# First halves of the next pass's tiles issued inside the attention, and output copies given to ScalarE there: a fused chunked-attention and snake-MLP kernel

## The chip, the cores and the metric

The kernel runs on one core of a Trainium2 chip. The metric is device time in microseconds (us) of the whole program. Six runs of the kernel before took 226.98 to 228.42 us, with a median of 227.48 us. One of the executions, the one that took 227.02 us, was also recorded by the hardware profiler. Its span from the first to the last instruction is 225.2 us, so 1.8 us lie around the span.

## The reference

Two operators follow one another. The first is attention in chunks: every chunk of 32 queries sees eight memory rows, 16 rows to its left, its own 32 and 8 to its right. The second is a two-layer MLP with the activation h + sin²(αh)/α.

```python
# B, H, S, D = 4, 8, 768, 64; chunk, left, right = 32, 16, 8
for c in range(S // chunk):
    l, r = max(0, c*chunk - left), min(S, (c+1)*chunk + right)
    kf = concat([mem_k, k[:, :, l:r]]); vf = concat([mem_v, v[:, :, l:r]])
    a = softmax(q_c @ kf.T / sqrt(D))
    out[:, :, c*chunk:(c+1)*chunk] = a @ vf
x = out.transpose(0, 2, 1, 3).reshape(3072, 512)
h = x @ w_in                       # 512 -> 2048
g = h + sin(alpha * h)**2 / (alpha + 1e-9)
return g @ w_out                   # 2048 -> 512
```

## The kernel before, in words

**Passes.** The batch has four elements, and each is a pass of 768 tokens: an attention that makes xT (the transposed attention output, 128 x 4 x 768, bf16), a first product with its activation (`layer`, 16 tiles of 128 hidden features each, which makes gT), and a second product (`second`, six output tiles of 128 tokens by 512). This text calls the attentions of passes 1, 2 and 3 A1, A2 and A3, and the layers after them layer 1, 2 and 3. Pass 0 has a different attention, `attention_first`, which the change doesn't touch.

**The order is written out by hand.** There is no scheduler: each engine executes its instructions in the order in which the program issues them. The second product is a generator, and `Feed.take(n)` issues its next n matmuls. So the second product of pass i runs in pieces inside the attention and the layer of pass i+1. In `attention` (line 448) the list `shares` says how many matmuls are taken in each step.

**A step of an attention.** Step s issues `scores(s)` (eight matmuls on TensorE and three exponentials on ScalarE, lines 270 and 283), half of the step's share of the feed, `values(s-2)` (eight matmuls, line 296, then a reciprocal and a multiplication on VectorE which make x_blk, lines 302 and 303), the other half of the share, and `turn_x(s-3)` (four transposes on TensorE, line 313, and a copy into xT on VectorE, line 316). There are eight blocks j = 0 to 7 of 96 tokens, and eleven steps. In A3 the first five blocks are not turned by TensorE: a transposing DMA, issued by SyncE (line 464), puts them into xT.

**A tile of a layer.** `first` issues `half_first` for tokens 0 to 383 (four matmuls, line 476, reading blocks 0 to 3 of xT) and for tokens 384 to 767 (blocks 4 to 7), then a sine on ScalarE (line 496). A square follows, on ScalarE (line 500) or on VectorE (line 503), as a string says: "VAVAVAVAAVAAVAVA" in layer 1, "AAAV" in layers 2 and 3. The fused multiply and add on VectorE that makes gT (line 506) is issued one tile later.

**PSUM.** There are eight banks. The planner `plan` gives names to sets of them, and `take_bank` hands out the one that was taken longest ago. In A1, A2 and A3, `big` holds three pairs of banks, which scores and values take in turn, and `one` holds two single banks. An output tile being accumulated keeps one of these (`kept`), and the transposes of `turn_x` use the other. The layer takes its pairs from `h`, which is `big`, and in layer 1 also the pair of `one`. A pair comes free when its last reader is done: the exponentials of line 283, the multiplication of line 303 or the fused add of line 506.

**Output tiles.** `end_o` (line 529) copies a finished bank into o_sb, which has two buffers. Even tiles are copied by VectorE (line 535), odd ones by ScalarE (line 537). SyncE then issues the output's DMA (line 538).

`ahead` (line 485) is already in the kernel: it takes a pair of `big`, issues the first half of tile ft into it and remembers the pair in `begun`, from which `layer` picks it up. Before, only `attention_first` calls it.

Of the kernel before, what the change touches and what calls it, by code (L numbers as in the profile page):

```python
# [42 lines left out]
def kernel(  # L43
# [17 lines left out]
    NJ = S // QW  # L61
# [17 lines left out]
    rings = {}  # L79

    def plan(**sets):
        for kind, ring in sets.items():
            rings[kind] = list(ring)
# [3 lines left out]
    def take_bank(kind):  # L87
        ring = rings[kind]
        bank = next(n for n in ring if n not in kept)
        ring.remove(bank)  # L90
        ring.append(bank)
        return bank

    def two(kind="big"):
        bank = take_bank(kind)
        return ps[:, bank:bank + 2, :]

    def single(kind="one"):
        return ps[:, take_bank(kind), :]

    def packed(bank, n, width):
        return bank.bitcast(BF)[:, 0:n * width].rearrange("p (n c) -> p n c", n=n)
# [54 lines left out]
    def cross_steps(b):  # L157
        for j in range(NJ):
            nc.sync.dma_start_transpose(kTs[b % 2][:, :, P * j:P * j + P], kst[:, j, :])
            yield  # L160
        for t in range(NSUB):
            nc.sync.dma_start_transpose(qTs[b % 2][:, :, P * t:P * t + P], qst[:, t, :])
            yield
# [31 lines left out]
    def send_memv(b):  # L195
        for j in range(NJ):
            nc.sync.dma_start(vws[b % 2][64:72, :, j, 0:D], memv_st[64:72, b])
# [62 lines left out]

    state = {"n": 0}

    def scores(b, j, kind="big"):
        pitch = 104 if b < 2 else P
        sc = two(kind)
        for hp in range(HP):
            for e in range(2):
                nc.tensor.matmul(  # L270
                    sc[:, e, QW * hp:QW * hp + QW],
                    kTs[b % 2][64 * e:64 * e + 64, hp, pitch * j:pitch * j + P],
                    qTs[b % 2][64 * e:64 * e + 64, hp, QW * j:QW * j + QW],
                )
        pt = pts[state["n"] % NPT]
        state["n"] += 1
        for m in range(3):
            col = m
            if j == 0 and m == 0:
                col = 3  # L280
            if j == NJ - 1 and m == 2:
                col = 4
            nc.scalar.activation(  # L283
                pt[:, 0:H * QW].rearrange("p (g e c) -> p g e c", g=2, e=4)[:, :, :, 32 * m:32 * m + 32],
                sc[:, :, 0:4 * QW].rearrange("p g (e c) -> p g e c", e=4)[:, :, :, 32 * m:32 * m + 32],
                ACTF.Exp, bias=biasm[:, col:col + 1], scale=0.125,
            )
        return pt

    def values(b, j, pt):  # L290
        ot = two()
        otv = ot[:, :, 0:4 * (D + 1)].rearrange("p e (g c) -> p e g c", c=D + 1)
        for e in range(2):
            for hp in range(HP):
                i = 4 * e + hp
                nc.tensor.matmul(  # L296
                    otv[:, e, hp, :], pt[:, QW * i:QW * i + P],
                    vws[b % 2][:, 2 * hp + e, j, 0:D + 1],
                )
        rinv = blk.tile([QW, 2, HP], F32, name="rinv")  # L300
        x_blk = blk.tile([QW, HP, 2, D], BF, name="x_blk", bufs=6)
        nc.vector.reciprocal(rinv[:], otv[0:QW, :, :, D])  # L302
        nc.vector.tensor_tensor(  # L303
            out=x_blk[:].rearrange("p g e d -> p e g d"), in0=otv[0:QW, :, :, 0:D],
            in1=rinv[:].unsqueeze(3).to_broadcast([QW, 2, HP, D]),
            op=ALU.mult,
        )
        return x_blk

    def turn_x(xT, j, x_blk):  # L310
        xtp = packed(single(), KT, QW)
        for kt in range(KT):
            nc.tensor.transpose(  # L313
                xtp[:, kt, :], x_blk[:, kt].rearrange("p e d -> p (e d)"), ident[0:QW, 0:QW]
            )
        nc.vector.tensor_copy(xT[:, :, QW * j:QW * j + QW], xtp)  # L316
# [131 lines left out]
    def attention(b, stream, shares, lag, crossed, beside=iter(()), beside_from=0):  # L448
        xT = xp.tile([P, KT, S], BF, name="xT")
        ptl, xbl = {}, {}  # L450
        for s in range(NJ + lag + 1):
            n = shares[s] if s < len(shares) else 0
            if s < NJ:
                ptl[s] = scores(b, s)
            if s == NJ - 1:
                nc.scalar.preload_act_table(ACTF.Sin)
            stream.take(n // 2)
            if s >= beside_from:
                next(beside, None)
            j = s - lag  # L460
            if 0 <= j < NJ:
                xbl[j] = values(b, j, ptl.pop(j))
                if j < crossed:
                    nc.sync.dma_start_transpose(
                        xT[:, :, QW * j:QW * j + QW], xbl.pop(j)[:].rearrange("p g e d -> p (g e d)")
                    )
            stream.take(n - n // 2)
            if crossed <= j - 1 < NJ:
                turn_x(xT, j - 1, xbl.pop(j - 1))
        return xT  # L470

    def half_first(hT, ft, hf, xT):
        for kt in range(KT):
            nc.tensor.matmul(  # L476
                hT[:, hf, 0:HALF],
                w_in_sb[:, kt, P * ft:P * ft + P],
                xT[:, kt, HALF * hf:HALF * hf + HALF],
                start=(kt == 0), stop=(kt == KT - 1),  # L480
            )
# [3 lines left out]
    def ahead(ft, hf, xT):  # L485
        if ft < 3:
            begun[ft] = two("big")
            half_first(begun[ft], ft, hf, xT)
# [24 lines left out]
    def second(i, gT, cut=0):  # L513

        def begin_o():
            bank = take_bank("one")
            kept.add(bank)
            return bank

        def part(s, bank, f0, f1):  # L520
            for ft in range(f0, f1):
                nc.tensor.matmul(  # L522
                    ps[:, bank, :], gT[:, ft, P * s:P * s + P], w_out_sb[:, ft, :],
                    start=(ft == 0), stop=(ft == FT - 1),
                )
                if ft < FT - 1:
                    yield

        def end_o(s, bank):
            kept.remove(bank)  # L530
            rings["one"].remove(bank)
            rings["one"].append(bank)
            o_sb = mlp.tile([P, d_model], F32, name="o_sb", bufs=2)
            if s % 2 == 0:
                nc.vector.tensor_copy(o_sb[:], ps[:, bank, :])  # L535
            else:
                nc.scalar.copy(o_sb[:], ps[:, bank, :])  # L537
            nc.sync.dma_start(out[S * i + P * s:S * i + P * s + P, :], o_sb[:])

        early = []  # L540
        if cut:
            for s in range(2):
                early.append(begin_o())
                yield from part(s, early[s], 0, cut)
        for s in range(NSUB):
            bank = early[s] if s < len(early) else begin_o()
            yield from part(s, bank, cut if s < len(early) else 0, FT)
            end_o(s, bank)
            yield
# [63 lines left out]
    xT = attention_first(kq, alphas, ahead)  # L613
# [62 lines left out]
    xT = attention(1, feed, (6, 8, 4, 4, 4, 3, 3, 3, 3, 1, 1), 2, 0, crossings, 3)  # L676
# [3 lines left out]
    for i in range(1, B):  # L680
        last = i == B - 1
        if i > 1:
            crossings = cross_steps(i + 1) if not last else iter(())

        def begin(ft, i=i):
            if ft == (2 if i > 1 else 0):
                for _ in crossings:
                    pass

        if i == 1:  # L690
            assert feed.left() == 16
            plan(h=rings["big"] + [min(rings["one"])])
            layer(i, xT, "VAVAVAVAAVAAVAVA", begin, 0)
            free = rings["h"]
            plan(one=(free[0], free[0] + 1), h=free[1:])
        else:
            plan(h=rings["big"])
            layer(i, xT, "AAAV", begin, feed.left() - (0 if last else 16))
        if not last:
            if i + 2 < B:  # L700
                load_rows(i + 2)
            plan(big=rings["h"])
            nc.scalar.preload_act_table(ACTF.Exp)
            feed.take(6)
            xT = attention(i + 1, feed, (4, 8, 4, 4, 3, 3, 3, 3, 4, 4, 4), 2, 5 if i == B - 2 else 0)
            if i + 2 < B:
                load_v(i + 2)
                send_memv(i + 2)
# [31 lines left out]
```

## Time and profile before

| | |
|---|---|
| median of six runs | 227.48 us (226.98 to 228.42) |
| profiled execution | 227.02 us, span 225.2 us |
| TensorE busy | 214.8 us, 95% of the span |
| ScalarE, VectorE, GpSimd busy | 151.7, 135.3, 84.2 us |
| granted TensorE clock, mean | 0.997 |
| A1, from its first score matmul to the first matmul of layer 1 | 61.32 to 78.20 us |
| layer 1, to the first matmul that follows it | 78.20 to 99.76 us |
| A2, likewise | 101.15 to 118.54 us |
| layer 2 | 118.54 to 148.65 us |
| A3 | 150.69 to 166.09 us |
| layer 3 | 166.09 to 199.60 us |
| last 100 matmuls of the second product | 199.60 to 221.27 us |

All positions are microseconds from the span's start, as the trace gives them. A row of the timeline has the start, the length, the engine, the line, what is computed and how many instructions are merged in it; in brackets stands how long the engine had been idle and which instruction ended that. A matmul's length includes the time until its result has arrived, so that matmuls which follow one another without a gap overlap in the rows. The time that a matmul takes of the engine is therefore read from start to start: eight matmuls of 128x384 from 118.71 to 120.04, some 0.163 us each, and 0.215 us for one of 128x512 (two from 120.04 to 120.47).

### The profile page before, as it was taken

Reading aid. Unit: us, or ns where it says so; the run is one execution under the profiler, and the core shown is the slowest. Engines: PE = TensorE matmul, PEld = TensorE weight load, DVE = VectorE, ACT = ScalarE, POOL = GpSimd, SP = SyncE. Lnnn points to the kernel's source line nnn. Section 1 sums busy time; section 2 is a strip of 40 time slices with the busy share of each in tenths; the row PEclk is TensorE's granted clock in tenths of the full one; section 3 lists DMA queues with packets and bytes.
Section 4 is the critical chain, followed back from the end, with each engine's and each line's share of the span. In section 5 each row is a group of like instructions: output and inputs, shape, how many; then the busy total and the mean of one; then the engine's idle time right before and its main releaser. Section 6 shows DMA issues by size and latency. Waiting matters only on the chain.

```text
span 225.2 us, 4455 instructions
## 1 busy us (share of the span) xinstructions
PE 214.8 (95%) x1720; PEld 115.9 (51%) x1720; DVE 135.3 (60%) x238; ACT 151.7 (67%) x222; POOL 84.2 (37%) x106
## 2 busy tenths in 40 slices
PE   7999999999998899999899999999999999999992
PEld 2555555555545555554555555544555555544440
DVE  5684748793526969995782775664743863771110
ACT  2559478894777579999856779798948678651011
POOL 7958843796979951175880000000000000000000
PEclk9999999999999999999999999999999999999998
DMA  5999999999999999999999954541330110111211
GB/s 79 163 117 136 170 210 208 206 204 139 93 209 168 130 118 175 117 138 132 159 177 102 99 104 93 103 156 54 68 108 3 47 47 0 48 51 47 93 66 74
DMA packets 94573, 25.97 MB, mean 115 GB/s; under 512 B 82632, under 2 KB 91480, under 8 KB 94552
## 3 DMA queue, kind: packets, MB, share of 16 engines
q0 software_dynamic: 71520, 14.81, 111.5%
q1 hardware_dynamic: 23032, 10.88, 23.7%
q8 instruction: 13, 0.21, 0.5%
q14 instruction: 8, 0.07, 0.2%
HBM read 29.67 MB, written 6.29 MB: 160 GB/s over the span
## 4 chain that ended last, share of the span: by engine, by line
PE 55%; DVE 8%; ACT 2%; issue 2%; DVEq 0%; ACTq 0%
PE ps L522 29%; PE ps L476 20%; DVE gT L506 3%; PE ps L270 2%; PE ps L296 2%; DVE u L503 2%; DVE x_blk L303 1%; ACT u L496 1%; PE ps L313 1%; ACT u L500 1%; DVE xT L316 1%; ACT o_sb L537 0%; DVE rinv L302 0%; DVE o_sb L535 0%; DVEq L506 0%
## 5 line engine op out<-in xcount | busy, mean ns | idle before, releaser
L522 PE MATMUL ps<-w_out_sb,gT 128*128 128x512 bf16 x384 | 99.3, 379 | 1.8 <-DVE o_sb L535 0.8
L476 PE MATMUL ps<-xT,w_in_sb 128*128 128x384 bf16 x512 | 90.0, 326 | 0.8 <-DVE gT L506 0.7
L506 DVE SCALAR_TENSOR_TENSOR gT<-u,inv_alpha,ps 128x768 bf16<-128x768 f32 x64 | 63.4, 1012 | 24.8 <-ACT u L500 20.6
L496 ACT ACTIVATE u<-ps,alpha_sb 128x768 f32<-128x768 f32 x64 | 57.0, 898 | 22.3 <-PE ps L476 21.2
L476 PEld LDWEIGHTS <-w_in_sb 128*128 128x128 bf16 x512 | 49.7, 98 | 37.6 <-issue 2.0
L522 PEld LDWEIGHTS <-gT 128*128 128x128 bf16 x384 | 34.2, 97 | 32.1 <-issue 2.1
L500 ACT ACTIVATE u<-u 128x768 f32<-128x768 f32 x40 | 33.7, 843 | 1.3
L283 ACT ACTIVATE pt<-ps,biasm 128x256 bf16<-128x256 f32 x72 | 28.7, 476 | 6.0 <-ACT pt L283 2.3
L535 DVE COPY o_sb<-ps 128x512 f32<-128x512 f32 x12 | 8.2, 687 | 24.8 <-PE ps L522 20.7
L537 ACT COPY o_sb<-ps 128x512 f32<-128x512 f32 x12 | 7.1, 589 | 22.2 <-PE ps L522 22.2
L503 DVE TENSOR_TENSOR u<-u 128x768 f32<-128x768 f32 x18 | 17.2, 954 | 6.0 <-ACT u L496 5.9
L303 DVE TENSOR_TENSOR x_blk<-ps,rinv 96x512 bf16<-96x512 f32 x24 | 16.5, 687 | 0.8
L144 POOL DMA_DIRECT2D kst<-in_k_dram x16 | 11.6, 724 | 9.9 <-DMA vw<-in_v_dram 4.4
L323 PE MATMUL ps<-idle 128*128 128x512 bf16 x39 | 13.7, 446 | 1.2 <-DVE vw L564 1.2
L139 POOL DMA_DIRECT2D kst<-in_k_dram x16 | 11.0, 686 | 7.7 <-DMA vw<-in_v_dram 5.5
L249 ACT COPY kT<-ps 128x672 bf16<-128x672 bf16 x8 | 5.8, 719 | 9.7 <-PE ps L234 6.8
L302 DVE RECIPROCAL rinv<-ps 96x8 f32<-96x8 f32 x24 | 4.9, 202 | 12.0 <-PE ps L296 6.1
L296 PEld LDWEIGHTS <-pt 128*128 128x128 bf16 x192 | 9.0, 98 | 4.8 <-issue 0.8
L503 POOL TENSOR_TENSOR u<-u 128x768 f32<-128x768 f32 x6 | 8.9, 1492 | 5.8 <-ACT u L496 5.8
L152 POOL DMA_DIRECT2D qst<-in_q_dram x12 | 10.5, 902 | 0.8 <-DMA kst<-in_k_dram 0.8
L296 PE MATMUL ps<-vw,pt 128*128 128x65 bf16 x192 | 9.8, 193 | 0.0
L270 PEld LDWEIGHTS <-kT 64*128 64x128 bf16 x192 | 4.9, 94 | 7.6 <-issue 7.0
(77 smaller groups left out, 154.0 us busy)
## 6 DMA issues: line engine op xcount, KB each, us to landing
out_dram<-o_sb SPq DMA_DIRECT2D x24, 256.0 KB
vw<-in_v_dram POOLq DMA_DIRECT2D x6, 384.0 KB, 13.4
w_out_sb<-in_moe_w_out_dram POOLq DMA_DIRECT2D x2, 1024.0 KB, 18.6
w_in_sb<-in_moe_w_in_dram POOLq DMA_DIRECT2D x3, 512.0 KB, 10.3
qst<-in_q_dram POOLq DMA_DIRECT2D x12, 128.0 KB, 6.4
kst<-in_k_dram POOLq DMA_DIRECT2D x14, 64.0 KB, 6.3
kst<-in_k_dram POOLq DMA_DIRECT2D x14, 56.0 KB, 6.6
k_bf<-in_k_dram POOLq DMA_DIRECT2D x4, 192.0 KB, 4.9
```

The source lines that it names most:

```text
L139: nc.gpsimd.dma_start(kst[r0:64, j, :].rearrange("p (h d) -> p h d", d=D), k[b, :, lo + r0:lo + 64, :].rearrange("h p d -> p h d"),)
L144: nc.gpsimd.dma_start(kst[72:72 + n, j, :].rearrange("p (h d) -> p h d", d=D), k[b, :, QW * j + 48:QW * j + 48 + n, :].rearrange("h p d -> ...
L283: nc.scalar.activation(pt[:, 0:H * QW].rearrange("p (g e c) -> p g e c", g=2, e=4)[:, :, :, 32 * m:32 * m + 32], sc[:, :, 0:4 * QW].rearra ...
L296: nc.tensor.matmul(otv[:, e, hp, :], pt[:, QW * i:QW * i + P], vws[b % 2][:, 2 * hp + e, j, 0:D + 1],)
L303: nc.vector.tensor_tensor(out=x_blk[:].rearrange("p g e d -> p e g d"), in0=otv[0:QW, :, :, 0:D], in1=rinv[:].unsqueeze(3).to_broadcast([Q ...
L323: nc.tensor.matmul(z, idle[:, 0:P], idle[:])
L476: nc.tensor.matmul(hT[:, hf, 0:HALF], w_in_sb[:, kt, P * ft:P * ft + P], xT[:, kt, HALF * hf:HALF * hf + HALF], start=(kt == 0), stop=(kt ...
L496: nc.scalar.activation(u[:], hT[:, :, 0:HALF], ACTF.Sin, scale=alpha_sb[:, ft:ft + 1])
L500: nc.scalar.activation(u[:], u[:], ACTF.Square)
L503: eng.tensor_tensor(out=u[:], in0=u[:], in1=u[:], op=ALU.mult)
L506: nc.vector.scalar_tensor_tensor(out=gT[:, ft, :].rearrange("p (e c) -> p e c", e=2), in0=u[:], scalar=inv_alpha[:, ft:ft + 1], in1=hT[:, ...
L522: nc.tensor.matmul(ps[:, bank, :], gT[:, ft, P * s:P * s + P], w_out_sb[:, ft, :], start=(ft == 0), stop=(ft == FT - 1),)
```

## The change

Three edits. In `attention`, three calls of `ahead` come in: tile 0 in the step of the last `values` (after its share of the feed and before that step's `turn_x`), tile 1 in the last step (after the first half of that step's share), and tile 2 after the last `turn_x`. While an attention is being issued (`state["attending"]`), `end_o` gives every output tile to ScalarE, not only the odd ones. Before layer 1 the pair of `one` goes to the front of `h` and not to its end, since tiles 0 to 2 have their pairs already and tile 3 is the first to take one from `h`.

```diff
     def attention(b, stream, shares, lag, crossed, beside=iter(()), beside_from=0):
         xT = xp.tile([P, KT, S], BF, name="xT")
         ptl, xbl = {}, {}
+        state["attending"] = True
         for s in range(NJ + lag + 1):
...
             j = s - lag
+            if j == NJ:
+                ahead(1, 0, xT)
             if 0 <= j < NJ:
                 xbl[j] = values(b, j, ptl.pop(j))
...
             stream.take(n - n // 2)
+            if j == NJ - 1:
+                ahead(0, 0, xT)
             if crossed <= j - 1 < NJ:
                 turn_x(xT, j - 1, xbl.pop(j - 1))
+        ahead(2, 0, xT)
+        state["attending"] = False
         return xT
...
             o_sb = mlp.tile([P, d_model], F32, name="o_sb", bufs=2)
-            if s % 2 == 0:
+            if s % 2 == 0 and not state["attending"]:
                 nc.vector.tensor_copy(o_sb[:], ps[:, bank, :])
             else:
                 nc.scalar.copy(o_sb[:], ps[:, bank, :])
...
-            plan(h=rings["big"] + [min(rings["one"])])
+            plan(h=[min(rings["one"])] + rings["big"])
```

More of the change, by code (lines that the diff above doesn't have):

```diff
@@ L259, in put_q @@
         )
-    state = {"n": 0}
+    state = {"n": 0, "attending": False}
     def scores(b, j, kind="big"):
```

## The prediction

> **What bounds the kernel now.** I read the page's busy times first, then the shares of the chain that ended last.
>
> ```profile
> PE 214.8 (95%) x1720; PEld 115.9 (51%) x1720; DVE 135.3 (60%) x238; ACT 151.7 (67%) x222; POOL 84.2 (37%) x106
> PE 55%; DVE 8%; ACT 2%; issue 2%; DVEq 0%; ACTq 0%
> ```
>
> TensorE (PE) is busy nearly everywhere and carries most of the chain. The change adds no matmul and takes none away: it can only fill holes on PE or make new ones. So the next view is what PE waits for (engine and line, releaser, total us, times, longest).
>
> ```profile
> PE ps L313 <- DVE xT L316: 0.9, 2, 0.6
> PE ps L522 <- DVE o_sb L535: 0.8, 1, 0.8
> PE ps L522 <- DVE xT L316: 0.6, 2, 0.3
> PE ps L313 <- ACT o_sb L537: 0.6, 1, 0.6
> PE ps L270 <- DVE gT L506: 0.2, 1, 0.2
> ```
>
> The first three rows are what the change aims at: the ends of the attentions (line 316) and one output copy on VectorE (line 535). PE's timeline shows them in place: the end of A1, the copy in A2, the end of A2. A3's end has the same hole as A2's, from 165.01 to 165.50.
>
> ```profile
> 76.24 0.38 PE L522 MATMUL ps<-w_out_sb,gT 128*128 128x512 bf16 x1
> 76.93 0.33 PE L313 MATMUL ps<-ident,x_blk 96*128 96x96 bf16 x4 [0.31 <-DVE xT L316]
> 77.10 0.38 PE L522 MATMUL ps<-w_out_sb,gT 128*128 128x512 bf16 x1
> 78.03 0.33 PE L313 MATMUL ps<-ident,x_blk 96*128 96x96 bf16 x4 [0.55 <-DVE xT L316]
> ...
> 110.82 0.34 PE L270 MATMUL ps<-qT,kT 64*128 64x96 bf16 x8
> 111.97 0.38 PE L522 MATMUL ps<-w_out_sb,gT 128*128 128x512 bf16 x1 [0.80 <-DVE o_sb L535]
> ...
> 117.04 0.60 PE L522 MATMUL ps<-w_out_sb,gT 128*128 128x512 bf16 x2
> 117.94 0.59 PE L522 MATMUL ps<-w_out_sb,gT 128*128 128x512 bf16 x2 [0.31 <-DVE xT L316]
> ```
>
> From start to start, less what the earlier group takes of PE (0.215 us per matmul of 512 columns, 0.28 for a group of scores), the holes are 0.47 and 0.72 us (A1), 0.87 (A2's copy), 0.47 (A2's end) and 0.49 (A3's end). Whether filling one shortens the program is a question for the stage behind it: busy times of layers 1, 2 and 3.
>
> ```profile
> core 0: us, PE busy (x) PEld busy (x) DVE busy (x) ACT busy (x) POOL busy (x), PEclk, DMA share, GB/s
> 80.68:103.54 22.86, 22.42 (x144) 12.63 (x142) 21.76 (x23) 21.93 (x27) 8.47 (x13) 1.00 2.28 135
> 118.54:150.70 32.16, 32.16 (x186) 17.53 (x183) 19.04 (x21) 25.64 (x30) 0.00 (x0) 1.00 1.37 106
> 166.09:199.60 33.51, 33.51 (x191) 18.30 (x189) 18.58 (x21) 24.10 (x28) 0.00 (x0) 1.00 0.09 33
> ```
>
> Layers 2 and 3 keep PE busy without a break, so what PE gains ahead of them reaches the end. Layer 1 has VectorE busy 21.76 of 22.86 us and PE waiting on it when A2 begins (102.67, the row of line 270). There a hole filled on PE is worth only what VectorE starts earlier.
>
> **Part 1, the end of A1.** After values(7) and its feed matmul at 76.24, PE now gets tile 0's half (4 x 0.163 = 0.65) at 76.46, transposes(6) at 77.11 (0.17), tile 1's half at 77.28, a feed matmul at 77.93, transposes(7) at 78.14, tile 2's half at 78.31. Every cover holds: blocks 0 to 3 of xT are copied by 74.33; the pairs were those of values 5, 6 and 7, read out by 75.52, 76.62 and 77.72; the copy of xT(6), 77.64 to 77.98, ends before 78.14. Both holes are gone, and tile 0's second half starts at 78.96, behind 1.30 us more of work, instead of 78.88. So the first sine comes 0.08 us later, at 79.82. Next is VectorE's stream. Before, its second fused add began at 82.86, 0.19 us after VectorE could have taken it, since the sine of tile 1 came only at 81.04; now that sine follows the first directly. Net: 0.08 late, 0.19 regained, **−0.11 us**. Bounds: +0.08 if the 0.19 isn't regained, −1.19 if both holes counted. I take −0.11, since the row of layer 1 shows VectorE without room.
>
> **Part 2, output copies.** Four even tiles move: two in A1, one each in A2 and A3; per copy, VectorE loses 687 ns and ScalarE gains 589 ns (page rows of lines 535 and 537), or 0.47 us until its next instruction starts (105.06 to 105.53).
>
> *A1, first copy.* On ScalarE it follows the exponentials that end at 64.58 and waits, as VectorE did until 64.17, for an output DMA that still reads the buffer. It runs from 64.47 to 65.06, before the next exponentials at 65.49: nothing. Behind it in ScalarE's queue are those exponentials, and values(1) waits for them. *A1, last copy.* It runs while ScalarE is idle, 76.51 to 79.74: nothing.
>
> *A2.* Tile 0's last matmul ends at 110.71. On VectorE the copy queued behind the multiplication of x_blk until 111.24; on ScalarE it starts in the tail of exponentials that end at 111.02, at about 110.90, and ends at 111.49. PE, which waits for that bank, goes on at 111.55, not 111.97: **−0.42**. The exponentials behind it slip by 0.11; values(5), which takes their bank pair, comes 0.6 us later still. Bounds: 0, if the copy ended only when VectorE's did, and −0.87, the whole hole.
>
> *A3.* Here no PE wait is removed: the next tile starts in the other bank, as there are no transposes between. But the copy lands in ScalarE's tightest stretch.
>
> ```profile
> 160.01 1.20 ACT L283 ACTIVATE pt<-ps,biasm 128x256 bf16<-128x256 f32 x3
> ...
> 161.35 0.41 PE L296 MATMUL ps<-vw,pt 128*128 128x65 bf16 x8
> ```
>
> Three pairs go round scores(5), values(3), scores(6), values(4), scores(7), values(5), so values(5), the matmuls at 161.35, need the exponentials of scores(6), which end at 161.21: 0.09 us of slack with 0.05 for the signal. With the copy ahead of them (159.82 on) they start at 160.29 and end at 161.49. PE waits until 161.54: **+0.19**, a wait that takes the place of none. Bounds: 0, if the copy overlaps more, and +0.55, if it counts in full.
>
> One rule of the Trainium skill speaks against this part: "ScalarE: Activation LUTs", Rules for kernel authors, gives cheap elementwise work to VectorE, up to about 3 times as fast in bf16. The rows here, fp32 read from PSUM, say 687 ns on VectorE and 589 on ScalarE. By the page a ScalarE copy would be 3 x 687 = 2.06 us (an estimate), A2 would lose 1.05 us instead of gaining 0.42, A3's wait would grow by 1.47, and the sum below would be +1.7 us. I go by the rows.
>
> SyncE's queue keeps its order: the output DMA in A1 goes out some 0.3 us later (64.89 before; its next entry is at 67.08), and in A3 it stands behind a transposing DMA until 162.24 in any case. GpSimd has nothing in the steps that are passed.
>
> **Part 3, the end of A2.** Tile 0's half starts at 116.87, then transposes(6), two feed matmuls, tile 1's half at 118.12, two feed matmuls at 118.77 (their bank, read by xT(6)'s copy, is free at 118.3), transposes(7) at 119.20, tile 2's half at 119.37. No hole is left: −0.47. What is late next is the pair for tile 3, which is tile 0's: its fused add ends 2.83 us after the first sine starts (120.07 and 122.90 before). That sine moves to 120.88, so the pair is free at 123.76; PE wants it at 123.69: +0.07. **−0.40**; bounds 0 and −0.47.
>
> **Part 4, the end of A3.** The same order. Blocks 0 to 3 of xT come by SyncE's DMAs, of which the fourth has been issued by 162.15; before, PE read them at 166.09 without a wait, now at 164.42. DMA traffic in the windows of half a microsecond falls from 0.62 (162.0 to 162.5) to 0.26, so I cost this at nothing; a landing after 164.42 would cost one for one. Tile 3 finds its pair with 0.6 us to spare, since 11 feed matmuls lie between (8 in layer 2). **−0.47**; bounds 0 and −0.49.
>
> **Part 5, the order of `h` before layer 1.** Tile 3 takes the pair of `one` as before: nothing.
>
> **Sum.** −0.11 −0.42 +0.19 −0.40 −0.47 = −1.21 us, against the profiled execution's 227.02 us (225.2 span and 1.8 around it): 225.81. That execution lies 0.46 us below the median of the runs; the same difference from the median gives 226.3.
>
> **Rivals.** *The holes of A1 count in full*: 1.08 us more, 225.2. For it: they are PE's largest group of waits at an attention's end, and PE is 98% busy in layer 1. Against: VectorE never idles there, and A2's second score group waits for its fused add.
>
> *The filled holes come back as waits*: at tile 3 in layers 2 and 3, or at the pairs that `ahead` takes. Then parts 3 and 4 yield nothing, the sum is −0.34, and the time 227.1. For it: 0.07 us is already missing in layer 2. Against: layer 3 has 0.6 us of room.
>
> *Slower: the first moved copy in A1 stops ScalarE.* On VectorE, waiting for the earlier output DMA delayed nobody; on ScalarE the exponentials are behind it, then values(1), then all of PE. Room is 0.43 us to the next exponentials and 0.57 more to values(1). A landing 0.35 + 1.0 + 1.21 = 2.6 us later than now turns the sum positive; 3.5 us later gives 228.4. For it: the DMA engines are busiest there, and that DMA took 5 us from its issue at 59.14. Against: the change doesn't touch it.
>
> **How the numbers follow.** Forecast, 226.3: 0.69, its own range 225.6 to 226.9 from the bounds of parts 2 to 4. Holes of A1 in full, 225.2: 0.08. Gain comes back, 227.1: 0.15. ScalarE stopped, slower: 0.08. The range 225.3 to 227.2 leaves the last case out, and a part of the ends. A measurement of this kernel tells 0.3% (0.68 us) from no change; the forecast is 0.53%. Faster: 0.64 of the forecast's 0.69 and the 0.08, 0.72; same: 0.05 + 0.14, 0.19; slower: 0.09 with a 0.01 of the third case.
>
> **What would show it.** Right: PE's wait list loses the rows of line 316 and of line 535; in A2 PE continues some 0.6 us after the last matmul of the tile has arrived, on a ScalarE copy; a new wait of 0.2 us of line 296 on line 283 in A3; PE's wait for VectorE at A2's second scores grows to more than 1 us. Wrong: A2 starts 1 us earlier; a wait of line 476 on line 506 at tile 3; values(1) waiting in A1; waits for DMA at line 476.

## The result, and the profile after

The changed kernel took 226.43 us (median of 18 runs, 225.64 to 227.98) against 227.41 us for the kernel before (39 runs). The ratio is 0.996, with a 95% interval of 0.9947 to 0.9972: 0.9 us faster, between 0.6 and 1.2. The forecast was 1.2 us. Two more executions on record, of 226.78 and 228.37 us, are not among the 18; with them the median is 226.45 us.

The profiled execution of the changed kernel took 226.88 us, with a span of 225.1 us, only 0.1 us less than the one before. A single span says little here: A1's first score matmul starts anywhere from 61.18 to 62.02 us in the profiles of this study, and the change alters no engine's order ahead of it. So the traces are compared in stretches that begin at that matmul.

PE's waits in the changed kernel (engine and line, releaser, total us, times, longest). Seven lines were added above most of the code, so that line 476 is now 483, 506 is 513, 522 is 529, 535 is 542 and 537 is 544.

```profile
PE ps L483 <- DVE gT L513: 1.5, 5, 0.5
PE ps L313 <- ACT o_sb L544: 0.6, 1, 0.6
PE ps L270 <- DMA qT<-qst: 0.6, 1, 0.6
PE ps L529 <- ACT o_sb L544: 0.4, 1, 0.4
```

The waits on xT's copies (line 316) are gone, and so is the one on VectorE's output copy. A wait of 0.4 us on ScalarE's copy has taken its place, as forecast. Two things are new. The tiles of layer 1 wait longer for VectorE: of the 1.5 us in the first row, 0.5 lie in pass 0, as in the kernel before, and 0.95 in four waits of layer 1, where before there was one of 0.15. And the first scores of A2 wait for a DMA. PE's timeline shows the ends of A1, A2 and A3 filled, and between them the waits that are left or new:

```profile
77.01 0.81 PE L483 MATMUL ps<-xT,w_in_sb 128*128 128x384 bf16 x4
77.66 0.34 PE L313 MATMUL ps<-ident,x_blk 96*128 96x96 bf16 x4
77.83 0.81 PE L483 MATMUL ps<-xT,w_in_sb 128*128 128x384 bf16 x4
78.48 0.38 PE L529 MATMUL ps<-w_out_sb,gT 128*128 128x512 bf16 x1
78.70 0.34 PE L313 MATMUL ps<-ident,x_blk 96*128 96x96 bf16 x4
...
83.43 2.76 PE L483 MATMUL ps<-xT,w_in_sb 128*128 128x384 bf16 x16 [0.50 <-DVE gT L513]
...
102.25 0.34 PE L270 MATMUL ps<-qT,kT 64*128 64x96 bf16 x8 [0.59 <-DMA qT<-qst]
...
112.37 0.38 PE L529 MATMUL ps<-w_out_sb,gT 128*128 128x512 bf16 x1 [0.38 <-ACT o_sb L544]
...
117.27 0.81 PE L483 MATMUL ps<-xT,w_in_sb 128*128 128x384 bf16 x4
117.91 0.34 PE L313 MATMUL ps<-ident,x_blk 96*128 96x96 bf16 x4
118.08 0.60 PE L529 MATMUL ps<-w_out_sb,gT 128*128 128x512 bf16 x2
118.52 0.81 PE L483 MATMUL ps<-xT,w_in_sb 128*128 128x384 bf16 x4
...
161.25 0.39 PE L529 MATMUL ps<-w_out_sb,gT 128*128 128x512 bf16 x1
161.70 0.40 PE L296 MATMUL ps<-vw,pt 128*128 128x65 bf16 x8
...
164.76 0.81 PE L483 MATMUL ps<-xT,w_in_sb 128*128 128x384 bf16 x4
```

From 77.01 to 78.70 and from 117.27 to 118.52 each group starts as the one before it ends. In layer 1 PE stands still before 83.43, waiting for a pair. At 161.70 `values(5)` comes 0.45 us after the start of a matmul that takes 0.215 us; the list of waits has no row for it, since a matmul's length in the rows covers most of the gap. The two rows of the kernel before that belong to this are its one wait in layer 1 and the hole at A3's end:

```profile
91.73 7.96 PE L476 MATMUL ps<-xT,w_in_sb 128*128 128x384 bf16 x48 [0.15 <-DVE gT L506]
...
165.50 0.59 PE L522 MATMUL ps<-w_out_sb,gT 128*128 128x512 bf16 x2 [0.31 <-DVE xT L316]
```

The cause of the gap before `values(5)` stands in ScalarE's timeline, where the copy lies ahead of the exponentials that `values(5)` needs:

```profile
65.02 0.59 ACT L544 COPY o_sb<-ps 128x512 f32<-128x512 f32 x1
...
111.72 0.59 ACT L544 COPY o_sb<-ps 128x512 f32<-128x512 f32 x1
...
159.95 0.59 ACT L544 COPY o_sb<-ps 128x512 f32<-128x512 f32 x1
160.41 2.33 ACT L283 ACTIVATE pt<-ps,biasm 128x256 bf16<-128x256 f32 x6
```

The copy at 65.02, the first that was moved, starts in the tail of the exponentials ahead of it, which end at 65.14: no output DMA holds it up.

One wait in VectorE's timeline of the changed kernel was not in the prediction:

```profile
150.40 0.69 DVE L542 COPY o_sb<-ps 128x512 f32<-128x512 f32 x1 [2.63 <-DMA out_dram<-o_sb]
151.00 1.00 DVE L513 SCALAR_TENSOR_TENSOR gT<-u,inv_alpha,ps 128x768 bf16<-128x768 f32 x1
```

The same copy before the change, of an output tile late in layer 2, had waited for its matmuls only:

```profile
149.52 0.69 DVE L535 COPY o_sb<-ps 128x512 f32<-128x512 f32 x1 [1.73 <-PE ps L522]
```

The copy is now 0.9 us later against a clock on which PE is no later at all (A3's first scores at 150.67, 150.69 before). The fused add behind it frees the pair that A3's second scores take. They start 1.39 us after the first ones; before, it was 1.25.

The stretches of all profiles, one execution of each kernel, worked out from the starts of the groups in the timelines: from A1's first scores to A2's second (before, VectorE frees their pair), on to A3's first, to A3's second, to `values(5)` of A3, and to the start of the last output copy.

| kernel | to A2's 2nd scores | to A3's 1st | to A3's 2nd | to values(5) | to the last copy |
|---|---|---|---|---|---|
| before | 41.35 | 48.02 | 1.25 | 9.41 | 59.92 |
| changed | 41.63 | 47.17 | 1.39 | 9.64 | 59.44 |
| e1, copies alone | 41.31 | 47.59 | 1.25 | 9.64 | 59.91 |
| e2, first halves alone | 41.63 | 47.60 | 1.71 | 9.41 | 59.44 |
| e3, A3's copy on VectorE | 41.25 | 47.17 | 1.47 | 9.41 | 59.45 |
| e4, A1 alone | 41.24 | 48.04 | 1.25 | 9.41 | 59.91 |
| e5, three output buffers | 41.24 | 47.17 | 1.25 | 9.63 | 59.40 |
| e6, e3 and e5 | 41.24 | 47.17 | 1.25 | 9.41 | 59.40 |
| e7, before, GpSimd squares | 41.45 | 48.27 | 1.25 | 9.41 | 59.92 |
| e8, changed, GpSimd squares | 41.03 | 47.47 | 1.65 | 9.63 | 59.44 |
| e9, changed, queries first | 41.25 | 47.17 | 1.24 | 9.64 | 59.44 |
| e10, e6, queries first | 41.25 | 47.17 | 1.25 | 9.41 | 59.40 |

Outside e7 and e8, a stretch changes only where its edit is in or out. Two things need a sentence of their own: the way to A3's second scores (below e5) and the 41.63 of the changed kernel (below e9). Otherwise the values repeat to 0.05 us from kernel to kernel. That is finer than the medians of whole runs can tell.

### The profile page after: what moved, and what is told of

Same layout as the page of the kernel before. It is cut to its first block, busy times and chain, and to the rows that moved or that the text cites. A ratio compares the mean times of both kernels' runs of the same rounds, so it can differ in the third digit from the quotient of the medians.

```text
span 225.1 us, 4458 instructions
## 1 busy us (share of the span) xinstructions
PE 215.2 (96%) x1720; PEld 116.1 (52%) x1720; DVE 133.1 (59%) x234; ACT 152.7 (68%) x226; POOL 84.4 (37%) x106
## 4 chain that ended last, share of the span: by engine, by line
PE 50%; DMA 9%; SPq 4%; ACT 2%; DVE 1%; issue 1%; ACTq 0%; DVEq 0%
PE ps L529 28%; PE ps L483 16%; DMA out_dram<-o_sb 5%; DMA qT<-qst 4%; SPq L162 3%; PE ps L296 2%; PE ps L270 2%; PE ps L313 1%; DVE gT L513 1%; ACT u L503 1%; ACT o_sb L544 1%; ACT u L507 0%; ACT pt L283 0%; SPq L197 0%; DVE o_sb L542 0%
## 5 line engine op out<-in xcount | busy, mean ns | idle before, releaser
L483 PE MATMUL ps<-xT,w_in_sb 128*128 128x384 bf16 x512 | 91.2, 326 | 1.6 <-DVE gT L513 1.5
L544 ACT COPY o_sb<-ps 128x512 f32<-128x512 f32 x16 | 9.4, 589 | 25.5 <-PE ps L529 25.5
L542 DVE COPY o_sb<-ps 128x512 f32<-128x512 f32 x8 | 5.5, 690 | 19.9 <-PE ps L529 17.2
L316 DVE COPY xT<-ps 128x384 bf16<-128x384 bf16 x19 | 6.6, 348 | 4.3 <-PE ps L313 4.3
```

The costliest lines, as they stand in the source:

```text
L483: nc.tensor.matmul(hT[:, hf, 0:HALF], w_in_sb[:, kt, P * ft:P * ft + P], xT[:, kt, HALF * hf:HALF * hf + HALF], start=(kt == 0), stop=(kt ...
```

## The experiments

The theory: the gain is made of A2's copy, A2's end and A3's end; A3 gives 0.2 us back; filling A1's holes is worth nothing, since VectorE sets layer 1. The rivals: A1's holes count; the gain comes back as waits; a wait in some queue that was passed.

### The two halves of the change: e1 and e2

e1 leaves `ahead` out of the attentions and `h` as before:

```diff
-            if j == NJ:
-                ahead(1, 0, xT)
...
-            if j == NJ - 1:
-                ahead(0, 0, xT)
...
-        ahead(2, 0, xT)
...
-            plan(h=[min(rings["one"])] + rings["big"])
+            plan(h=rings["big"] + [min(rings["one"])])
```

> The output copies alone: even tiles go to ScalarE inside the attentions, no first halves come forward. By the forecast A2 gains 0.42 us (PE goes on at a ScalarE copy) and A3 loses 0.19 to 0.23 (values(5) waits for exponentials behind the copy), so 0.2 us faster than the kernel before, a ratio of 0.999. If the copies were the whole gain of the change, it would be 0.9 us faster, 0.996; if ScalarE were held up by the output DMA in A1, it would be slower.

Measured: ratio 0.9992 (0.9977 to 1.0008). The interval holds the forecast and zero, and leaves out 0.996. The stretches tell it more finely: 0.43 gained in A2 (47.59 against 48.02), 0.23 lost in A3 (9.64 against 9.41).

e2 leaves the copies as before:

```diff
-            if s % 2 == 0 and not state["attending"]:
+            if s % 2 == 0:
```

> The first halves alone, with the output copies as before. By the forecast A2's and A3's ends gain 0.40 and 0.47 us. In A1 the last output copy stays on VectorE between the copies of xT(6) and xT(7), and now comes later, since its last matmul stands behind tile 0's and tile 1's halves: xT(7) ends some 0.4 us later, and layer 1 starts 0.3 us later than before. So 0.6 us faster than before, 0.997. If the holes of A1 counted in full, 1.7 us faster, 0.993.

Measured: 0.9977 (0.9961 to 0.9992), 0.5 us faster; 1.7 us is out. A2's second scores come 0.28 us later (41.63 against 41.35), as worked out. The copy stands where the text put it, in VectorE's timeline of e2:

```profile
78.46 0.69 DVE L542 COPY o_sb<-ps 128x512 f32<-128x512 f32 x1 [0.37 <-PE ps L529]
79.07 0.35 DVE L316 COPY xT<-ps 128x384 bf16<-128x384 bf16 x1
```

So A1's last copy, which the prediction costed at nothing, must be moved if A1's first halves are: not for its own 0.69 us, but because it would now stand behind them and ahead of xT(7). A3's second scores start 0.46 us late in e2; e1 has nothing of that. The loss comes with the first halves.

### A3's copy: e3

```diff
-        state["attending"] = True
+        state["attending"] = b < 3
```

> The changed kernel, with A3's even output copy left on VectorE. By the forecast the wait of values(5) on the exponentials in A3 goes, 0.2 us, and nothing else changes: 1.1 us faster than before, 0.995. If that wait is hidden by what follows, the time is that of the changed kernel, 0.996.

Measured: 0.9946 (0.9928 to 0.9965), 1.2 us faster. `values(5)` is back at 9.41. In whole runs the 0.2 us against the changed kernel lies within the intervals; in the stretch it is 0.23 us, and e6 repeats it.

### A1 alone: e4

```diff
-        state["attending"] = True
+        state["attending"] = b == 1
...
-            if j == NJ:
+            if j == NJ and b == 1:
                 ahead(1, 0, xT)
...
-            if j == NJ - 1:
+            if j == NJ - 1 and b == 1:
                 ahead(0, 0, xT)
...
-        ahead(2, 0, xT)
+        if b == 1:
+            ahead(2, 0, xT)
```

> Only A1's part of the change: first halves and copies in A1, all else as before. By the forecast VectorE's stream in layer 1 begins the same and wins 0.11 us, so A2 starts 0.1 us earlier and the ratio is 1.000 (same). If A1's holes count in full, 1.2 us faster, 0.995. If what layer 1 and A2 wait for is SyncE's queue (the transposing DMAs of the next queries), as the profile of the changed kernel has it, 0 to 0.4 us slower.

Measured: 0.9988 (0.9974 to 1.0002), 0.27 us faster with zero just inside the interval, and 1.2 us far outside. Both holes of A1 are filled here, 1.19 us of PE, and A2's second scores come 0.11 us earlier (41.24 against 41.35), the forecast's figure. Whole runs can't tell 0.11 us from nothing; that much rests on the stretches.

### The late output copy: e5 and e6

e5 gives the output tiles three buffers; the room is taken from x_blk. The other tiles that share these buffers are set alike.

```diff
-            o_sb = mlp.tile([P, d_model], F32, name="o_sb", bufs=2)
+            o_sb = mlp.tile([P, d_model], F32, name="o_sb", bufs=3)
...
-        x_blk = blk.tile([QW, HP, 2, D], BF, name="x_blk", bufs=6)
+        x_blk = blk.tile([QW, HP, 2, D], BF, name="x_blk", bufs=4)
```

> The changed kernel with three output buffers in place of two (room made by four buffers of x_blk in place of six). In the profiles with first halves at A2's end (the change, e2, e3) an output copy on VectorE late in layer 2 starts 1 us late, waiting for an output DMA that SyncE issued late, and PE then waits 0.14 to 0.40 us at A3's second scores. With three buffers that copy waits for nothing, and the loss goes: 0.2 us less than the changed kernel, 1.1 us faster than before, 0.995. If that wait is a chance of single executions, nothing changes, 0.996.

Measured: 0.9933 (0.9920 to 0.9946), 1.5 us faster. In VectorE's timeline of e5 the copy waits for its matmuls again:

```profile
148.76 0.69 DVE L542 COPY o_sb<-ps 128x512 f32<-128x512 f32 x1 [1.72 <-PE ps L529]
```

A3's second scores are back at 1.25. The wait was no chance: it is in the profiles of all five kernels that have first halves at A2's end and two buffers (changed, e2, e3, e8, e9), where the copy cost PE between nothing (e9) and 0.46 us (e2), and in none of the others. Where it comes from is read in SyncE's queue, in the kernel before:

```profile
118.28 0.33 SPq L538 DMA_DIRECT2D out_dram<-o_sb  x1
...
147.17 3.40 SPq L538 DMA_DIRECT2D out_dram<-o_sb  x3
```

and in the changed one:

```profile
119.33 0.33 SPq L545 DMA_DIRECT2D out_dram<-o_sb  x1
...
148.06 3.39 SPq L545 DMA_DIRECT2D out_dram<-o_sb  x3
```

The last output DMA of A2 goes out 15.61 us after A2's second scores before (118.28 − 102.67) and 15.83 us after (119.33 − 103.50): tile 0's first half, 0.65 us, stands ahead of that tile's last matmuls, and the tile's copy and DMA wait for them. Behind this DMA SyncE issues eight copies of memory values and 14 transposing DMAs until 147 or 148, and only then the outputs of layer 2. The third of these tiles needs the buffer of the first. So from A2's second scores SyncE comes to these outputs as late as before (44.56 us, 44.50 before), while PE reaches A3's first scores 0.85 us sooner (47.17, 48.02) and wants the buffer sooner.

What e5 shows is the buffer: with a third one the wait and the loss are gone. That the pushed matmuls keep the queue late is read from the queue and has no run of its own. The kernels that differ by the halves fit it: without them SyncE comes to the outputs at 43.87 us (e1, 44.56 in the changed kernel), with them at 45.31 (e2, 44.50 before). But from the issue of A2's last output DMA to layer 2's first, the queue takes 27.4 to 29.1 us in the twelve profiles. Before the eighth copy of memory values alone the queue stands 1.1 to 3.1 us; in the kernel before it is 3.0 us, put down by the profile to an output DMA. How large the loss is in one execution is therefore not set by the push alone.

e6 is e3 and e5 together.

> Both costs taken out: A3's even copy stays on VectorE, and there are three output buffers (four of x_blk). If both are real and independent, 1.4 us faster than before, 0.994, with no wait of line 296 on line 283 in A3 and none of A3's second scores on VectorE. If only the first is, 1.2 us, 0.995.

Measured: 0.9928 (0.9915 to 0.9941), 1.6 us faster than before, with both stretches at the shortest values of the table. It beats both kernels: the changed one's interval begins at 0.9947, and e6's ends at 0.9941.

### Relieving VectorE in layer 1: e7 and e8

Both edits, on the kernel before (e7) and on the changed one (e8):

```diff
-            layer(i, xT, "VAVAVAVAAVAAVAVA", begin, 0)
+            layer(i, xT, "VAPAVPAAPAVAPAVA", begin, 0)
```

P stands for GpSimd. The call that sends the memory values for A2 moves behind the loop over the transposing DMAs of A2's queries:

```diff
     load_v(2)
-    send_memv(2)
...
                 for _ in crossings:
                     pass
+                if i == 1:
+                    send_memv(2)
```

> The kernel before, with four of layer 1's squares given to GpSimd (three from VectorE, one from ScalarE), and SyncE's copies of the memory values put behind the transposing DMAs of the next queries, so that these can't bind. VectorE's stream in layer 1 falls from 22.9 to about 20 us, ScalarE's from 22 to 21. If VectorE's stream sets the start of A2, A2's second scores come some 0.8 us earlier, with ScalarE or PE next, 0.9965. If the start of A2 hangs on something else, 1.000 or above.

> The same two edits on the changed kernel. If VectorE's stream is what kept A1's filled holes from counting, they count now in part, until ScalarE binds: 1.1 us at A2's start and 0.9 us behind it, 2.0 us faster than the kernel before, 0.991, and 1.2 us less than e7. If the holes are worth nothing for another reason, the distance to e7 is 0.9 us, as between the changed kernel and the one before.

Measured: e7 1.0015 (1.0003 to 1.0027), slower; e8 0.9974 (0.9960 to 0.9988). In both the gain that was hoped for did not come, and by the number the other branch did: 1.000 or above for e7, and for e8 a distance to e7 of 0.95 us (227.73 and 226.78), where 0.9 was said for holes that are worth nothing. That decides little, since the edit did not do what it was for. VectorE's work became less, but its stream hardly shorter, as the window from its first square to the end of its last fused add in layer 1 of e8 shows:

```profile
core 0: us, PE busy (x) PEld busy (x) DVE busy (x) ACT busy (x) POOL busy (x), PEclk, DMA share, GB/s
80.61:103.03 22.42, 21.28 (x135) 11.75 (x134) 19.09 (x20) 20.67 (x25) 11.55 (x12) 1.00 1.97 124
```

It is busy 19.09 of 22.42 us (DVE; in the changed kernel 21.67 of 22.89), and idles because a square takes GpSimd 1.46 us and more: before the second pair of fused adds of e8 VectorE waits 1.01 us for one. The kernel also issues the fused add of a tile that GpSimd squares one tile later than that of the others (`layer`), so that such a tile keeps its pair longer. So this didn't relieve layer 1. Between e7 and e8 A2's second scores move by 0.42 us, more than the 0.11 us of e4; but the loss at A3's second scores takes 0.40 us back. In both kernels VectorE no longer sets these scores: they follow the first ones after 1.25 us, without a wait (1.52 us with one before and in e4). ScalarE does not follow: its exponentials start 0.65 us after A2's second scores, where it was 0.23 us before and in e3, and the next stretch is 0.25 and 0.30 us longer than in the kernels without these squares.

One rival is left open by this. In layer 1 ScalarE is as full as VectorE (21.93 and 21.76 of 22.86 us before). That VectorE sets the layer is read from the waits: its rows there show a single idle time, 0.27 us for ScalarE, while in the changed kernel ScalarE waits 0.34 and 0.29 us for PE, and PE for VectorE. No run relieves VectorE alone.

### The wait for A2's queries: e9 and e10

e9 has the second edit of e8 alone, e10 has it on e6.

> The changed kernel with one edit in SyncE's order: the transposing DMAs of A2's queries go ahead of the copies of the memory values, some 8 us earlier. In the changed kernel's profile PE waited 0.59 us for them at A2's first scores, in the other three profiles with first halves in A1 (e2, e3, e4) not. If that wait is common, the kernel is 0.2 to 0.4 us faster than the changed kernel: 1.2 us faster than before, 0.995. If it is rare, the time is the changed kernel's, 0.996.

> Three output buffers, A3's even copy on VectorE, and the query transposes first. If the wait for the queries is common, 0.2 to 0.4 us less than e6, 0.9915; if rare, e6's time, 0.993.

Measured: 0.9964 (0.9950 to 0.9979) and 0.9926 (0.9912 to 0.9939), the same as the changed kernel and as e6. So the 0.59 us at A2's first scores in the changed kernel's profile is rare: none of the other profiles has it. It lengthened that execution by 0.38 us (41.63 against 41.25 in e9); in the medians no price of it can be seen.

## Why the prediction was right

The measured time lies in the range, and the gain is three quarters of the forecast. By its steps:

- **Part 1, A1's end, −0.11 us.** Shown: 41.24 or 41.25 against 41.35 in e3 to e6, e9 and e10; e4's whole runs leave out the rival in which A1's holes count in full. VectorE's first square comes 0.08 us later after A1's first scores (81.31 − 61.87 against 80.68 − 61.32), and its first two fused adds take 0.19 us less, both as worked out:

```profile
81.74 2.13 DVE L506 SCALAR_TENSOR_TENSOR gT<-u,inv_alpha,ps 128x768 bf16<-128x768 f32 x2
...
82.37 1.94 DVE L513 SCALAR_TENSOR_TENSOR gT<-u,inv_alpha,ps 128x768 bf16<-128x768 f32 x2
```

The first row is of the kernel before. One sign that the prediction named did not come: PE's wait for VectorE at A2's second scores was to grow to more than 1 us. It is 0.21 us in e3, e4, e5 and e9, as before, and in the changed kernel's profile the wait for the queries stands in its place. PE is held up earlier, at the pairs of layer 1. From start to start, at 1.30 us for eight matmuls, the layer loses 1.83 us of PE in the changed kernel (120 matmuls from 78.87 to 100.20) and 0.76 us before (128 from 78.20 to 99.76): 1.07 of the 1.19 us come back there. And "VectorE never idles there" was too strong: its own row left 1.10 of 22.86 us without work.

- **Part 2, A2's copy, −0.42.** Shown by e1: −0.43. The copy took 0.59 us on ScalarE, against 0.69 us on VectorE. So for this fp32 copy out of PSUM the rows held, and the threefold advantage that the Trainium skill ("ScalarE: Activation LUTs", Rules for kernel authors) gives VectorE in bf16 did not carry over to it.
- **Part 2, A3's copy, +0.19.** Shown by e1, which has it, and by e3 and e6, which take it out: 0.23. The argument by the order in which three pairs of banks go round held.
- **Part 2, A1's copies, nothing.** Right for the first, which waited for no DMA. For the last one right as the change stands; e2 shows that with the first halves it costs 0.38 us left where it was (41.63 against 41.25).
- **Part 3, A2's end, −0.40, and part 4, A3's end, −0.47.** Measured −0.42 (e2) and −0.48 (59.44 against 59.92). No wait for xT's transposing DMAs in A3 appeared. At tile 3 of layer 2 PE starts 0.05 us late (124.18; three matmuls from 123.48 end 0.65 us later), where the sum had 0.07; in layer 3 it does not wait.
- **The term that was wrong: SyncE's queue, costed at nothing.** The prediction followed the output DMAs of the copies that move. It did not follow the one whose copy stays on ScalarE, but whose matmuls were pushed behind tile 0's half at A2's end. It missed that the transposing DMAs and later the outputs of layer 2 stand behind it on SyncE, and that two output buffers tie VectorE to that queue, so that PE's gain in A2 meets a buffer that comes free no sooner. In the profiles this costs 0.14 us in the changed kernel, nothing in e9 and up to 0.46 in e2. e5 shows the buffer as the cause; what keeps the queue late is in part argued, as said there.

The measured terms of the changed kernel are −0.11 − 0.43 + 0.23 − 0.42 − 0.48 + 0.14 = −1.07 us; with a loss as in e2 it would be −0.75. The whole runs gave −0.9. In e5, which is the changed kernel without that loss, the stretches come to −1.27 against the kernel before, near the forecast's sum, and whole runs give 1.5 us with an interval from 1.2 to 1.8. The rival in which the gain comes back as waits was right in kind, but in another place, and with at most 0.46 of its 0.87 us.

## What to carry to other kernels

When work is moved forward on one engine, follow what it overtakes to the end of the overtaken work's chain, not only to the engine's next wait: here a copy, its DMA, 22 entries of SyncE's queue behind that, and a buffer 30 us later. A filled hole counts where the stage behind it is bound by the same engine: here 1.19 us of PE ahead of a stage in which PE waits for VectorE were worth 0.11 us, while holes of 0.47 and 0.49 us ahead of stages that PE sets were worth 0.42 and 0.48. And single stretches between fixed points of the trace repeat here to 0.05 us, where the runs of one kernel spread over more than 1 us (225.64 to 227.98), so they can show what the medians can't.

## What the runs showed that was not expected

Squares given to GpSimd took 2.6 us of work off VectorE in layer 1 (19.19 us busy in e7, 21.76 before) and made the kernel before slower (1.0015). Single fused adds behind them waited up to 1.32 us for GpSimd, and the first two stretches of e7 became 0.10 and 0.25 us longer.

An output tile's DMA that SyncE issued at 148.06 let its buffer be written again only at 150.40, 2.3 us later, and it is the same 2.3 us in e2, e3, e8 and e9. (In A1 of the kernel before it took 5.0 us, from 59.14 to 64.17.) With two buffers, an output that is issued late is therefore felt by the engine that fills the buffer: before the change, with the issue at 147.17, the copy came at 149.52, 2.35 us later, and found its buffer free just in time.
